# The y of the second mixture's second group, and the first block of the tail, moved in among the expert items

## The chip, the cores and the metric

The kernel runs on one core of a Trainium2 chip. The metric is the device time of one execution in microseconds (us). Engines are named as in the profile: PE is TensorE, DVE VectorE, ACT ScalarE, POOL GpSimd, SP SyncE; PEld is TensorE's loading of weights. Each engine works through its own queue in order.

## The reference

Three stages follow each other: attention in a sliding window, a mixture of eight experts, and a wide layer with g(h) = h cos h ("second mixture" here). All is float32, and the weights of the last layer come as float64.

```
x = softmax(mask(q k^T / 8 - slope |i - j|)) v        # 4 batches, 8 heads, 576 rows, window 128
x = x as 2304 rows of 512
e = argmax(x w_gate + modality_bias[modality_id])     # 8 experts
out[t] = gate[t] * (relu(x[t] w1[e]) w2[e])           # w1 512 x 1024, w2 1024 x 512
h = out w_in                                          # 512 x 2048
y = (h * cos(h)) w_out                                # 2048 x 512
```

## The kernel before

Every product of two float32 matrices is made of three: each operand is split into a high half, a cast to fp32r, and a low half, the rest; TensorE then does high x high, high x low and low x high. A split is so always a cast on ScalarE and a subtraction on VectorE.

**The expert items.** After attention the 2304 rows are sorted by expert into nine items of up to 256 rows each, and a remainder of blocks of up to 128 rows. The loop over `steps` (line 1087) has 72 steps, (item, f) with f over the eight slices of 128 hidden columns, and two more that only finish. Step n does the up products of slice f (`up`, twelve products of 256 columns, tiles `xT` and `s`) and, LAG = 2 steps behind, the down products (`down`, twelve, tiles `hh` and `s`). Two slices make a piece of weights: `load_w` loads `r1` and `r2` (512 KB each, two buffers of each), `split_w1` and `split_w2` split them into `s1s` (three tiles) and `s2s` (two). After a piece's second up, `hh` gets its high half (relu on ScalarE) and low half (VectorE). At an item's end `store_y` copies its four banks and stores y; the place in DRAM is known only at run time, so a later read of y waits for every earlier store. Among the steps 10 to 56 `convert` also turns the first half of the second mixture's float64 weights into `wi_a` and `wo_a` (`from_f64`, line 101: mag and lf on ScalarE, top on VectorE, lf times mag on GpSimd). From step 12 to 66 (`InOrder`) the instructions of each engine stand as the code has them; later a scheduler places them.

**The first block** (`unit_parts`, line 902) is the remainder's first, 128 rows with the roles turned: x is the stationary operand and products have 512 columns. `load_d(p)` loads one eighth of the expert's weights (p 0 to 3 from w1, 4 to 7 from w2), `split_d(p)` splits it into `sds[p]`, `up_d(p)` does six products; after p = 1 and p = 3 the hidden half is taken out with relu (`hr`), `turn` transposes it on TensorE and splits it into `hh2`, `down_d(p)` does six products of the second layer, `end` transposes and stores. The raw weights go to five tiles `raw` of their own; the splits stand at steps 70 to 73, up_d from step 72 on, the rest behind the loop. Other blocks run in a loop of which the count is read at run time (line 1152); here it is not entered.

**The second mixture.** The rows are in five groups of 512 (the last of 256). For group g `fetch_y` (line 861) loads a 128-row tile of y and its gates (`yg`, `gb`), `load_y` (line 868) multiplies them on GpSimd and splits the product into `yT`. In segments of a group and half the weights, `up2` does twelve products of 512 columns (`yT`, `wi_a` or `wi_b`) and the chain of h cos h: ki on ScalarE, two steps of r on VectorE, abs and sin on ScalarE, a product on VectorE, then `gg`, high half on ScalarE and low half on VectorE. `down2` does twelve products two steps behind (`wo_a`, `gg`). The second half of the weights, `wi_b` and `wo_b`, is converted during the first three segments. Before the change group 0 is fetched in steps 66 to 69 of the items, group 1 in the second mixture's own first steps.

## Time and profile before

| what | us |
|---|---|
| runs of the kernel | 871.32, 872.38, 876.11 (median 872.38) |
| the profiled execution | 872.53 |
| its span, first to last instruction | 870.8 |
| TensorE busy in it | 823.5 (95%) |
| VectorE busy | 631.9 (73%) |
| ScalarE busy | 529.2 (61%) |
| GpSimd busy | 223.4 (26%) |
| mean granted TensorE clock | 0.987 |

Times in the rows are us from the span's start. The items run from about 200 to 437 us, the first block ends at 454, the second mixture fills the rest. A start in an order of time is where an instruction began; "x12" are twelve that were merged, and what is in brackets is the time that the engine stood idle before it and what ended that.

### The profile page before, as it was taken

The numbers are of one execution on the slowest core, as the hardware profiler recorded it, in microseconds if no ns is written. First come the engines' busy times: TensorE is split into PE (matmuls) and PEld (weight loads), VectorE is DVE, ScalarE is ACT, GpSimd is POOL, SyncE is SP. The second block draws the span as 40 slices with busy tenths as digits, with TensorE's granted clock in tenths as the row PEclk, the third lists the DMA queues.
The fourth block names the chain that finished last, engine by engine and source line by source line (L and its number), as shares of the span: only waits on it lengthen the run. The fifth ranks groups of instructions, "written<-read, shape, count | busy, mean of one in ns | idle before, by whom it ended". The sixth has DMA issues, their size and how long they took to land. (4 is left out here: it accounts for less than half of the span.)

```text
span 870.8 us, 14990 instructions
## 1 busy us (share of the span) xinstructions
PE 823.5 (95%) x5269; PEld 728.1 (84%) x5269; DVE 631.9 (73%) x1492; ACT 529.2 (61%) x980; POOL 223.4 (26%) x283
## 2 busy tenths in 40 slices
PE   6899999987989999999987999999999999999996
PEld 6789988976889999999966888887788888888895
DVE  4877778767879999897646999998665565545562
ACT  6988788844556666664535776664544555445562
POOL 6665565320112223221113211111313001200000
PEclk9999999997999999999998999999999999999999
DMA  7354442018578877856824131410402000100000
GB/s 159 95 139 110 117 109 75 32 42 261 182 254 263 299 269 266 277 197 208 293 85 140 51 132 60 153 65 25 133 19 91 1 1 21 53 1 0 25 26 24
DMA packets 125137, 103.43 MB, mean 119 GB/s; under 512 B 61725, under 2 KB 105027, under 8 KB 125059
## 3 DMA queue, kind: packets, MB, share of 16 engines
q1 hardware_dynamic: 122099, 92.74, 34.6%
q0 software_dynamic: 2960, 9.70, 3.2%
q8 instruction: 42, 0.69, 0.3%
q14 instruction: 36, 0.29, 0.1%
HBM read 85.90 MB, written 16.52 MB: 118 GB/s over the span
## 5 line engine op out<-in xcount | busy, mean ns | idle before, releaser
L973 PE MATMUL bk<-hh,s 128*128 128x256 f32 x864 | 121.8, 287 | 7.9 <-DVE hh L973 7.1
L973 PEld LDWEIGHTS bk<-hh,s 128*128 128x128 f32 x864 | 109.7, 191 | 12.0 <-DVE hh L973 10.3
L973 PE MATMUL bk<-xT,s 128*128 128x256 f32 x864 | 117.2, 285 | 1.4 <-ACT s L973 0.9
L973 PE MATMUL bk<-wo_a,gg 128*128 128x512 f32 x432 | 110.0, 402 | 4.4 <-ACT gg L973 3.8
L973 PEld LDWEIGHTS bk<-xT,s 128*128 128x128 f32 x864 | 109.9, 193 | 1.9 <-ACT s L973 1.0
L973 PE MATMUL bk<-yT,wi_b 128*128 128x512 f32 (+1 forms) x480 | 107.3, 372 | 0.0
L973 PE MATMUL bk<-yT,wi_a 128*128 128x512 f32 (+1 forms) x480 | 106.3, 372 | 0.5 <-PEq L1152 0.5
L973 DVE TENSOR_TENSOR s<-r,s 128x1024 fp32r<-128x1024 f32 x72 | 93.6, 1303 | 17.8 <-ACT s L973 17.4
L973 PE MATMUL bk<-wo_b,gg 128*128 128x512 f32 x432 | 104.9, 392 | 0.5 <-ACT gg L973 0.3
L973 ACT ACTIVATE r<-r 128x512 f32<-128x512 f32 (+1 forms) x80 | 47.1, 589 | 94.8 <-DVE r L973 94.4
L973 POOL TENSOR_TENSOR lf<-lf,mag 128x512 f32<-128x512 f32 x32 | 46.3, 1446 | 218.8 <-DVE mag L973 194.1
L973 PEld LDWEIGHTS bk<-wo_a,gg 128*128 128x128 f32 x432 | 81.9, 192 | 24.0 <-ACT gg L973 4.7
L973 ACT CAST s<-r 128x1024 fp32r<-128x1024 f32 x72 | 75.3, 1052 | 42.4 <-DMA r<-in_moe_w_dram 33.8
L973 PEld LDWEIGHTS bk<-yT,wi_a 128*128 128x128 f32 x480 | 85.0, 190 | 17.5 <-ACTq L1152 0.7
L973 PEld LDWEIGHTS bk<-yT,wi_b 128*128 128x128 f32 x480 | 84.8, 188 | 17.6
L973 PEld LDWEIGHTS bk<-wo_b,gg 128*128 128x128 f32 x432 | 80.5, 188 | 19.2 <-ACT gg L973 0.8
L973 DVE TENSOR_TENSOR r<-bk,r 128x512 f32<-128x512 f32 (+1 forms) x80 | 51.0, 637 | 60.2 <-ACT r L973 59.8
L973 DVE TENSOR_TENSOR gg<-r,gg 128x512 fp32r<-128x512 f32 (+1 forms) x80 | 55.9, 699 | 36.8 <-ACT gg L973 36.5
L973 ACT CAST gg<-r 128x512 fp32r<-128x512 f32 (+1 forms) x80 | 46.1, 577 | 46.6 <-DVE r L973 45.4
L712 PE MATMUL bk<-vt,pT 128*128 128x65 f32 x544 | 71.8, 275 | 1.9 <-POOL pT L686 0.8
L712 PEld LDWEIGHTS bk<-vt,pT 128*128 128x128 f32 x544 | 67.8, 195 | 3.2 <-issue 1.5
L973 DVE SCALAR_TENSOR_TENSOR r<-ki,bk 128x512 f32<-128x512 int32 (+1 forms) x80 | 50.5, 631 | 23.6 <-ACT ki L973 23.3
(279 smaller groups left out, 1380.0 us busy)
## 6 DMA issues: line engine op xcount, KB each, us to landing
r<-in_moe_w_dram SPq DMA_DIRECT2D x72, 512.0 KB
f64w<-in_moe_w_in_dram SPq DMA_DIRECT2D x14, 512.0 KB
f64w<-in_moe_w_out_dram SPq DMA_DIRECT2D x13, 512.0 KB
y_dram<-y SPq DMA_DIRECT2D x19, 256.0 KB
yg<-y_dram SPq DMA_DIRECT2D x18, 256.0 KB
rqk<-in_q_dram SPq DMA_DIRECT2D x32, 128.0 KB
rqk<-in_k_dram SPq DMA_DIRECT2D x32, 128.0 KB
vt<-in_v_dram SPq DMA_DIRECT2D x32, 128.0 KB
```

The costliest lines, as they stand in the source:

```text
L712: nc.tensor.matmul(ot[:, h, 0:65], pT[b], vt_of(bp, t0 + b, hg)[:, 65 * h:65 * h + 65], start=b == 0, stop=b == nv - 1)
L973: r = op(*args, **kwargs)
```

## The change

Five things are moved.

1. `load_y` of group 0 goes from steps 68 to 71 to steps 46 to 49, and group 1's from the second mixture to steps 66 to 69. The fetches stand two steps ahead of each (44 and 64). The tile `yT1` takes the memory that `raw` had.
2. The block's raw weights use the items' own buffers `r1` and `r2`: four buffers for eight loads, `load_d` at steps 66, 67, 68 and 70, the other four as a split frees a buffer.
3. `split_d` of p = 0 and 1 stand at steps 68 and 70, `up_d` of p = 0 and 1 at steps 70 and 71, the next two and `turn(0)` among steps 72 and 73. `hr` is kept in the tiles `xgs`, which held gathered x.
4. The second mixture opens with four up products; then two down products, and from there it is two steps behind as it was. The banks for h are four in turn instead of three. The first two float64 conversions there wait two steps longer after their load.
5. The copies of partial sums that go to DRAM are all on ScalarE; half were on VectorE.

```diff
-        nc.sync.dma_start(raws[p % len(raws)], src.rearrange("o (j p) d -> p (o j) d", p=128))
+        r = RAW["d", p] = rp_.tile([128, 2, DM], F32, name="rd", tag="r%d" % (1 + p // 2 % 2), bufs=2)
+        nc.sync.dma_start(r, src.rearrange("o (j p) d -> p (o j) d", p=128))
...
+    sds = sds[:4] + sds[:3] + sds[4:]
...
-        w, r = sds[p % len(sds)], raws[p % len(raws)]
+        w, r = sds[p], RAW.pop(("d", p))
...
-        if p + len(raws) < 8:
-            load_d(p + len(raws))
+        if p < 4:
+            load_d(p + 4)
...
-                hr[h] = gp.tile([128, DM], F32, name="hr", tag="y")
+                hr[h] = xgs[1 - h]
...
-        return [part((up_d, 0)), part((up_d, 1)), part((split_d, 4), (up_d, 2), (split_d, 5), (turn, 0)),
-                part((up_d, 3), (split_d, 6)), part((down_d, 4), (split_d, 7), (turn, 1)), part((down_d, 5)),
-                part((down_d, 6)), part((down_d, 7)), part((end,))]
+        return {"begin": [part((up_d, 0)), part((up_d, 1))],
+                "among": [(part((split_d, 2), (split_d, 3), (turn, 0)), part((up_d, 2), (split_d, 4))),
+                          (part(), part((up_d, 3), (split_d, 5)))],
+                "end": [part((down_d, 4), (turn, 1), (split_d, 6), (split_d, 7)), part((down_d, 5)), part((down_d, 6)),
+                        part((down_d, 7)), part((end,))]}
...
-        N0, N1 = len(steps) - 5, len(steps) - 10
+
+        N0, N1, N2 = 44, len(steps) - 10, len(steps) - 8
...
-        SPLIT_AT = [-2, -1, 0, 1]
         first = unit_parts()
+        LOAD_AT, SPLIT_AT, BEGIN_AT = {66: 0, 67: 1, 68: 2, 70: 3}, {68: 0, 70: 1}, (70, 71)
...
-            if 0 <= n - N0 + 1 < groups[0][1]:
-                fetch_y(0, n - N0 + 1, gp)
-            if 0 <= n - N0 - 1 < groups[0][1]:
-                load_y(0, n - N0 - 1, ytiles[0])
+            for g, n0 in enumerate((N0, N2)):
+                if 0 <= n - n0 < groups[g][1]:
+                    fetch_y(g, n - n0, gp)
+                if 0 <= n - n0 - 2 < groups[g][1]:
+                    load_y(g, n - n0 - 2, ytiles[g])
...
-            if n >= len(steps):
-
-                first.pop(0)()
+
+            if n in SPLIT_AT:
+                split_d(SPLIT_AT[n])
+            if n in BEGIN_AT:
+                first["begin"].pop(0)()
+            among = first["among"].pop(0) if n >= len(steps) else (lambda: None,) * 2
+            among[0]()
             if n >= LAG:
                 down(*steps[n - LAG])
+            among[1]()
+            if n in LOAD_AT:
+                load_d(LOAD_AT[n])
...
-        conv = Steps([lambda f=f, fn=fn, w=w: fn(NA + f, w[1][:, 0, f], w[1][:, 1, f], cv, f64w, 0)
-                      for f, fn, w in turns if 0 <= f < NA])
+        conv = Steps([lambda n=n, f=f, fn=fn, w=w: fn(NA + f, w[1][:, 0, f], w[1][:, 1, f], cv, f64w, 2 if n < 2 else 0)
+                      for n, (f, fn, w) in enumerate(t for t in turns if 0 <= t[0] < NA)])
...
-            ph = bank("SST"[i % 3], [128, 512])[:, :w]
+            ph = bank("SSTT"[i % 4], [128, 512])[:, :w]
...
-                        (nc.scalar.copy if j % 2 else nc.vector.tensor_copy)(o, ACC[s][j])
+                        (nc.scalar.copy if j % 2 or f1 < NF2 else nc.vector.tensor_copy)(o, ACC[s][j])
...
-            if i >= LAG and (s < NS - 1 or f < LAG or f >= TAIL):
+
+            if i > LAG and (s < NS - 1 or f < LAG or f >= TAIL):
+                if i == LAG + 1:
+                    down2(*downs.pop(0))
                 ins = down2(*downs.pop(0))
```

What this does to the order on the engines is shown at three places. The first is VectorE in steps 46 to 49 (s1 and s2 are halves of the items' weights, hh the hidden tile that TensorE waits for, mag, top and wo_a belong to a float64 conversion). Before:

```order
L973 TENSOR_SCALAR mag_5711<-top_5752 128x512
L973 TENSOR_TENSOR s1_1_3776<-r1_5745,s1_1_3776 128x1024
L973 TENSOR_TENSOR top_5752<-top_5752,wo_a_3767 128x512
L132 TENSOR_TENSOR wo_a_3767<-top_5752,lf_5753 128x512
L973 SCALAR_TENSOR_TENSOR hh_5844<-bk_5797,hh_5844 128x512
L973 TENSOR_TENSOR s2_0_3778<-r2_5674,s2_0_3778 128x1024
L973 TENSOR_SCALAR mag_5830<-mag_5830 128x512
L973 TENSOR_SCALAR top_5862<-mag_5830 128x512
L973 SCALAR_TENSOR_TENSOR top_5862<-f64w0_3789,top_5862 128x512
L973 TENSOR_TENSOR s1_2_3777<-r1_5822,s1_2_3777 128x1024
L973 TENSOR_SCALAR mag_5830<-top_5862 128x512
L973 SCALAR_TENSOR_TENSOR hh_5914<-bk_5869,hh_5914 128x512
```

and after:

```order
L974 TENSOR_SCALAR mag_5711<-top_5756 128x512
L974 TENSOR_TENSOR yT0_3771<-yg_5733,yT0_3771 128x4x128
L974 TENSOR_TENSOR s1_1_3776<-r1_5749,s1_1_3776 128x1024
L974 TENSOR_TENSOR top_5756<-top_5756,wo_a_3767 128x512
L974 SCALAR_TENSOR_TENSOR hh_5859<-bk_5805,hh_5859 128x512
L974 TENSOR_TENSOR yT0_3771<-yg_5785,yT0_3771 128x4x128
L132 TENSOR_TENSOR wo_a_3767<-top_5756,lf_5757 128x512
L974 TENSOR_TENSOR s2_0_3778<-r2_5674,s2_0_3778 128x1024
L974 TENSOR_SCALAR mag_5845<-mag_5845 128x512
L974 TENSOR_SCALAR top_5884<-mag_5845 128x512
L974 SCALAR_TENSOR_TENSOR top_5884<-f64w0_3789,top_5884 128x512
L974 TENSOR_TENSOR yT0_3771<-yg_5818,yT0_3771 128x4x128
```

Three of four splits of y (yT0) stand in these rows, the fourth right behind the next hh; each waits for a product on GpSimd. The end of the float64 weight (wo_a) now stands behind the hh that it was ahead of.

The second is TensorE from step 70 to the branch (xT_94 and hh with 256 columns are the last item, s with xT_95 and 512 columns is up_d, s with hh and a number is down_d, ident are the transposes of turn and end). Before:

```order
L973 MATMUL bk<-xT_94,s_2_3777 128x256 x12
L973 MATMUL bk<-hh,s_0_3778 128x256 x12
L973 MATMUL bk<-s_0_3775,xT_95 128x512 x6
L973 MATMUL bk<-hh,s_1_3779 128x256 x12
L973 MATMUL bk<-s_1_3776,xT_95 128x512 x6
L973 MATMUL bk<-hh,s_1_3779 128x256 x12
L973 MATMUL bk<-s_2_3777,xT_95 128x512 x6
L973 MATMUL bk<-ident,hr 128x128 x4
L973 MATMUL bk<-s_0_3778,xT_95 128x512 x6
L973 MATMUL bk<-s_1_3779,hh_6872 128x512 x6
L973 MATMUL bk<-ident,hr 128x128 x4
L973 MATMUL bk<-s_0_3775,hh_6872 128x512 x6
```

and after:

```order
L974 MATMUL bk<-xT_94,s_2_3777 128x256 x12
L974 MATMUL bk<-s_0_3775,xT_95 128x512 x6
L974 MATMUL bk<-hh,s_0_3778 128x256 x12
L974 MATMUL bk<-xT_94,s_2_3777 128x256 x12
L974 MATMUL bk<-s_1_3776,xT_95 128x512 x6
L974 MATMUL bk<-hh,s_0_3778 128x256 x12
L974 MATMUL bk<-ident,xg_97 128x128 x4
L974 MATMUL bk<-hh,s_1_3779 128x256 x12
L974 MATMUL bk<-s_2_3777,xT_95 128x512 x6
L974 MATMUL bk<-hh,s_1_3779 128x256 x12
L974 MATMUL bk<-s_0_3778,xT_95 128x512 x6
L974 MATMUL bk<-s_0_3775,hh_6851 128x512 x6
```

The two first sets of up_d stand between the last item's own products, and no set of transposes is followed at once by the products that need it.

The third is ScalarE after the branch, at the opening of the second mixture (ki, r and gg are the chain of h cos h; mag and lf belong to the float64 weights). Before:

```order
L973 ACTIVATE ki<-bk 128x512
L973 ACTIVATE r<-r 128x512
L973 ACTIVATE r<-r,hpi 128x512
L973 ACTIVATE ki<-bk 128x512
L973 ACTIVATE mag<-f64w 128x512
L973 CAST gg<-r 128x512
L973 ACTIVATE mag<-f64w 128x512
L973 ACTIVATE ki<-bk 128x512
L973 ACTIVATE r<-r 128x512
```

and after:

```order
L974 ACTIVATE ki<-bk 128x512
L974 ACTIVATE lf<-f64w 128x512
L974 ACTIVATE r<-r 128x512
L974 ACTIVATE r<-r,hpi 128x512
L974 ACTIVATE ki<-bk 128x512
L974 CAST gg<-r 128x512
L974 ACTIVATE ki<-bk 128x512
L974 ACTIVATE r<-r 128x512
L974 ACTIVATE r<-r,hpi 128x512
```

The two mag are gone from these rows, and one lf stands right behind the first ki.

## Rows read from the trace of the kernel before

**Rows 1.** Stretches: us of it; busy us (instructions) of five engines; granted clock; DMA.

```profile
346.00:368.00 22.00, 21.52 (x180) 21.11 (x179) 21.09 (x30) 15.13 (x22) 6.95 (x5) 1.00 0.82 275
...
427.00:455.00 28.00, 23.12 (x136) 18.76 (x135) 16.66 (x19) 13.01 (x20) 5.85 (x4) 1.00 0.38 120
455.00:482.00 27.00, 22.56 (x84) 17.42 (x83) 17.45 (x28) 14.00 (x24) 7.14 (x5) 0.87 0.40 123
```

**Rows 2.** TensorE's waits from 425 to 480: us in total, times, longest.

```profile
PE bk L973 <- ACT gg L973: 3.8, 2, 3.1
PE bk L973 <- ACT hr L973: 1.8, 2, 1.1
```

**Rows 3.** Order of time on TensorE, step 70 to the branch: start, us, operation.

```profile
427.03 1.58 PE L973 MATMUL bk<-xT,s 128*128 128x256 f32 x12
...
438.42 1.59 PE L973 MATMUL bk<-hh,s 128*128 128x256 f32 x12
439.85 1.55 PE L973 MATMUL bk<-s,xT 128*128 128x512 f32 x6
...
448.09 0.60 PE L973 MATMUL bk<-ident,hr 128*128 128x128 f32 x4
448.44 4.38 PE L973 MATMUL bk<-s,hh 128*128 128x512 f32 x18
...
454.65 8.41 PE L973 MATMUL bk<-yT,wi_a 128*128 128x512 f32 x36 [0.46 <-PEq L1152]
```

**Rows 4.** Order of time on SyncE around the branch.

```profile
454.95 0.37 SPq L946 DMA_DIRECT2D y_dram<-y  x1
458.69 0.39 SPq L144 DMA_DIRECT2D f64w<-in_moe_w_in_dram  x1
```

**Rows 5.** Order of time on ScalarE, opening of the second mixture.

```profile
459.79 0.63 ACT L973 ACTIVATE r<-r 128x512 f32<-128x512 f32 x1 [1.48 <-DVE r L973]
...
462.52 0.67 ACT L973 ACTIVATE mag<-f64w 128x512 f32<-128x512 f32 x1 [0.86 <-DMA f64w<-in_moe_w_in_dram]
463.10 0.60 ACT L973 CAST gg<-r 128x512 fp32r<-128x512 f32 x1
467.38 0.66 ACT L973 ACTIVATE mag<-f64w 128x512 f32<-128x512 f32 x1 [3.67 <-DMA f64w<-in_moe_w_in_dram]
```

**Rows 6.** Order of time on TensorE, opening of the second mixture.

```profile
472.69 0.73 PE L973 MATMUL bk<-wo_a,gg 128*128 128x512 f32 x2 [3.12 <-ACT gg L973]
...
478.48 3.71 PE L973 MATMUL bk<-yT,wi_a 128*128 128x512 f32 x12
482.03 2.95 PE L973 MATMUL bk<-wo_a,gg 128*128 128x512 f32 x12
484.81 2.89 PE L973 MATMUL bk<-yT,wi_a 128*128 128x512 f32 x12
```

**Rows 7.** The stretch right behind the longest gap, columns as in rows 1.

```profile
474.00:476.00 2.00, 1.95 (x5) 1.58 (x6) 1.97 (x4) 1.31 (x3) 0.20 (x1) 0.50 0.07 21
```

**Rows 8.** The tile yg: duration in ns (least, median, longest), first and last start.

```profile
L973 POOL TENSOR_TENSOR yg<-yg,gb x18: 1283/1292/2052, 429.7 to 745.2; 128x512 f32<-128x512 f32 x18
...
L973 DVE TENSOR_TENSOR yT<-yg,yT x18: 678/684/1121, 431.6 to 790.4; 128x512 fp32r<-128x512 f32 x18
```

**Rows 9.** Groups of instructions, 340 to 400 us: busy us, mean ns, idle before.

```profile
L973 DVE TENSOR_TENSOR s<-r,s 128x1024 fp32r<-128x1024 f32 x19 | 25.9, 1363 | 3.3 <-ACT s L973 3.2
...
L973 DVE TENSOR_TENSOR top<-top,wo_a 128x512 f32<-128x512 f32 x7 | 5.9, 837 | 0.0
```

**Rows 10.** Order of time on VectorE, steps 46 to 52.

```profile
357.85 1.78 DVE L973 TENSOR_TENSOR top<-top,wo_a 128x512 f32<-128x512 f32 x1
359.74 0.69 DVE L132 TENSOR_TENSOR wo_a<-top,lf 128x512 fp32r<-128x512 f32 x1
...
370.25 1.23 DVE L973 TENSOR_TENSOR s<-r,s 128x1024 fp32r<-128x1024 f32 x1 [1.86 <-ACT s L973]
```

**Rows 11.** Order of time on ScalarE, step 51.

```profile
369.17 1.05 ACT L973 CAST s<-r 128x1024 fp32r<-128x1024 f32 x1 [2.06 <-DMA r<-in_moe_w_dram]
```

More of the change, by code (lines that the diff above doesn't have):

```diff
@@ L874, in load_y @@
         nc.vector.tensor_tensor(yT[:, 1, :, cs], yg, yT[:, 0, :, cs].bitcast(F32), op=ALU.subtract)
-    ctx_d = ctx.enter_context(ExitStack())
-    raws = []
     def load_d(p):
@@ L938, in end @@
             r = nc.sync.value_load(regs[0:1, NL + MIN_ITEMS:NL + MIN_ITEMS + 1], min_val=0, max_val=NT)
-            yr = gp.tile([128, DM], F32, name="hr", tag="y")
+            yr = xgs[1]
             nc.scalar.copy(yr, acc[0])
@@ L984 @@
     nc = Engines
+    rps = hc.enter_context(ExitStack())
+    rp_ = pool(rps, "rp", 2, "right")
     with ExitStack() as c:
-        rps = c.enter_context(ExitStack())
-        rp_ = pool(rps, "rp", 2, "right")
         cvs = c.enter_context(ExitStack())
@@ L1120 @@
                 cvs.close()
-                dp = pool(ctx_d, "dp", 1)
-                raws += [dp.tile([128, 2, DM], F32, name=f"raw{j}") for j in range(5)]
-            if N1 < n <= N1 + len(raws):
-                load_d(n - N1 - 1)
+                yt1 = pool(ctx, "yt1", 1)
+                ytiles.append(yt1.tile([128, 2, KD * 512], F32R, name="yT1"))
             if n == len(steps) - 1:
                 splits(len(pieces), len(pieces))
-            if n - len(steps) in SPLIT_AT:
-                split_d(SPLIT_AT.index(n - len(steps)))
-            if n >= len(steps):
-                first.pop(0)()
+            if n in SPLIT_AT:
[4 more added lines that the diff above has]
+            among[0]()
             if n >= LAG:
                 down(*steps[n - LAG])
+            among[1]()
+            if n in LOAD_AT:
+                load_d(LOAD_AT[n])
             with ExitStack() as later:
@@ L1141 @@
                     convert(n)
-        for part in first:
+        for part in first["end"]:
             part()
         InOrder.on = False
-        rps.close()
     n_units = nc.values_load(regs[0:1, 2 * NL:2 * NL + 1], min_val=0, max_val=UNITS,
@@ L1160 @@
             gather(MIN_ITEMS, 0)
-            for p in range(len(raws)):
+            for p in range(4):
                 load_d(p)
             to_xT(MIN_ITEMS, 0)
-            for p in range(4):
+            parts = unit_parts()
+            for p in range(2):
                 split_d(p)
-            for part in unit_parts():
+            for part in parts["begin"] + [p for two in parts["among"] for p in two] + parts["end"]:
                 part()
@@ L1170 @@
     rc.close()
-    ctx_d.close()
-    yt1 = pool(ctx, "yt1", 1)
-    ytiles.append(yt1.tile([128, 2, KD * 512], F32R, name="yT1"))
     with ExitStack() as c:
@@ L1270 @@
             for j in range(groups[g][1]):
-                if s and (s == 1 or f0 == 0):
-                    at = 0 if s == 1 else i0 - 8
-                    fetches.setdefault(at + j, []).append((g, j))
-                    loads.setdefault(at + 2 + j, []).append((g, j))
+                if g > 1:
+                    fetches.setdefault(i0 - 8 + j, []).append((g, j))
+                    loads.setdefault(i0 - 6 + j, []).append((g, j))
                 if f0:
```

## The prediction

> **What bounds the kernel now.** I read the busy times by stretch first, then TensorE's waits, then the order of time on TensorE, ScalarE, VectorE and SyncE around them. TensorE is the bound nearly everywhere, so a change pays only where TensorE stands idle or runs at a lower clock, and costs wherever it makes TensorE wait anew. The stretches [rows 1] tell two stories. From 346 to 368 us (steps 44 to 50 of the items) TensorE is busy 21.52 of 22 us and VectorE 21.09: two engines full at once. From 427 to 455 us (end of the items and the first block) TensorE is idle 4.9 us, and from 455 to 482 us (opening of the second mixture) 4.4 us, with the granted clock at 0.87 on average. The longest waits there [rows 2] are 3.8 us for the high half of gg and 1.8 for the block's hidden values (hr). The change is aimed at these stretches.
>
> **The block, steps 70 on.** TensorE starts step 70 at 427.03 and the mixture at 454.65 [rows 3]: 27.6 us. Twelve 256-column products take 1.43 us at full pace (438.42 to 439.85 [rows 3]), six 512-column ones 1.39 (half of twelve, 482.03 to 484.81 [rows 6]), four transposes 0.35 (448.09 to 448.44 [rows 3]). The stretch holds six of the first (8.6), eight of the second (11.1) and three of the third (1.1): 20.8. So 6.8 us are lost: the gaps, and the drain of the pipeline at each. After the change two up products stand between the items' own, and turn(0) and turn(1) have other products around them, so relu, cast and split hide beside 1.4 us or more of products. What stays is the end (the shorter of the two waits for hr, 0.7 [rows 2], and 0.46 at the branch [rows 3], with drain some 1.7). What is new: the first split needs a load that leaves only at step 66, behind item 7's stores and a fetch of y that needs them landed. Step 65 ends near 415.2 (four steps of 2.86 and one transposition before 427.03). The second copy of y now stands on ScalarE behind a split that waits for its own load, so I put the second store at 418.5, an estimate. SyncE passes on 3.7 us after a store (454.95 to 458.69 [rows 4]), so 422.2, and the load leaves at about 422.8. A load of 512 KB takes 3.8 us (458.69 until ScalarE has it at 462.52 [rows 4, 5]): 426.6, up to 427.5 with others in flight. A cast of 1.05 [rows 11] and a split of 1.23 [rows 10] give the low half at 428.9 to 429.8, where TensorE wants it at 428.9: 0 to 0.9, I take 0.8. The eighth load waits until the fourth split has freed its buffer, and the last split then makes the second hidden tile late by some 1.4 us. With 0.2 at the first turn the new loss is 1.7 + 0.8 + 1.4 + 0.2 = 4.1 us. **Gain 6.8 - 4.1 = 2.7 us.** Bounds: 5.1 (only the end stays) and 0.3 (the loads 2.4 us later, two thirds of a load's length).
>
> **The opening.** From 454.65 [rows 3] to the fourth set of down products at 482.03 [rows 6] TensorE does seven sets of twelve, 84 products of 512 columns. At 2.78 us a set that is 19.5 us; it takes 27.4. Of the lost 7.9, 4.4 are gaps, one of them 3.12 long [rows 6], and after it the granted clock stands at 0.50, the lower of the two levels [rows 7]: a set of up products takes 3.55 us there (478.48 to 482.03), and some 6 us at half pace lose 3.1. The gaps come from ScalarE: its abs for the second float64 weight (mag) waits for a load until 467.38 [rows 5] and holds everything of the second and third gg behind it. Now the fetches of y that were in that load's way have moved, the two abs stand later, and four sets of up products cover 11.1 us. One wait is new: ScalarE has the low words of the first float64 weight (lf) right behind the first ki, before the first r. SyncE sends that load only at 458.69, 4.0 us after the branch, and it is there at 462.52, 7.9 after. Without the wait r starts at 459.79, 5.1 after the branch; with a lf like the mag of 0.67 it starts 8.5 after. From r's start to the end of the first gg it took 3.9 us, of which mag waited 0.86 and stood 0.58 in the way [rows 5]; so 2.5 to 3.1, and gg's high half comes 11.0 to 11.6 after the branch, where TensorE wants it at 11.1. The second gg follows along the same chain some 4.4 us later, at 15.6, an estimate; TensorE is done with the first down set at 14.2. So the waits are 0.3 and 1.4, with drains and a late low half 2.4 in all. **Gain 7.9 - 2.4 = 5.5 us**, if the clock stays up: the block's gaps of up to 1.1 us left it at 1.00 [rows 1, 2], the one of 3.12 did not. Bounds: 7.2 (load early) and 2.4 (clock falls: 3.1 less).
>
> **The items.** Eight load_y now lie among the items: the first four in steps 46 to 49, the second four in 66 to 69, where VectorE has room. In the first place it has none, idle 0.9 us of 22 [rows 1]. Each load_y adds 1.29 us on GpSimd and 0.68 on VectorE [rows 8], 0.60 from start to start. And GpSimd's products hold VectorE up where both inputs lie in SBUF: the top at 357.85 takes 1.78 us instead of 0.69 [rows 10], and over 340 to 400 us the 19 splits take 1363 ns instead of 1220, the seven such tops 837 instead of 690 [rows 9], in sum 3.7 us for six products of GpSimd, 0.6 each. So VectorE gets 4 x 0.60 + 4 x 0.6 = 4.8 us more before the hh of steps 46 to 50. It can give back the 1.86 us of idle time at 370.25 [rows 10], which ended with a cast that had waited 2.06 us for weights [rows 11], and TensorE's slack at one hh, an estimated 0.5: TensorE ends 2.4 us later. This is not won back, TensorE being the bound after it. The fetches (1 MB), whose second pair waits on SyncE for the first pair's split, delay weights by a microsecond or two within this. At step 61 one cast of y stands ahead of an hh on ScalarE: 0.4 more. **Loss 2.8 us.** Bounds: 0.8 (idle time takes most of it) and 6.5 (nothing given back, and a load late by 1.3).
>
> By the Trainium skill (SBUF — State Buffer, Who interferes with whom) the pair of ports that the two engines share is locked for a whole instruction, so the later one blocks fully. The rows agree with it in kind. Taken at its worst, each of GpSimd's products would block VectorE its whole length, and the forecast would come out 2.8 us higher.
>
> The rest is at nothing: copies of partial sums moved to ScalarE, which is busy 14.0 of 27 us from 455 to 482 [rows 1] while TensorE has products to do; a fourth bank in the later segments, which moves products on TensorE but adds none; hidden tiles in the xgs buffers, which are read out by then.
>
> **Sum**, against the profiled execution's own 872.53 us (span 870.8; the median of the runs is 872.38, 0.15 lower): 872.53 - 2.7 - 5.5 + 2.8 = 867.1 us, 0.6% below the median. About 0.5%, 4.4 us, is what a measurement here can tell from no change: faster is under 868.0, slower over 876.7.
>
> **Rivals.**
> (1) The items hide the load of y: loss 0.8, and block gain 3.5. Then 872.53 - 3.5 - 5.5 + 0.8 = 864.3. For it: VectorE's splits run up to two pieces ahead. Against: TensorE waits for hh right there, and VectorE has 0.9 us free. Chance 0.25.
> (2) The wait for lf takes the place of the one for mag: the first gg comes later than four sets cover, TensorE stands long enough that the clock falls again, opening gain 2.4: 870.2. For it: the load cannot leave before 458.69. Against: 11.1 us of cover. Chance 0.17.
> (3) The change does not do what it says, the block begins no sooner in effect: its loads queue behind stores and fetches, each up product waits, block gain 0.3: 869.5. For it: eight loads now pass through four buffers, two of a kind. Chance 0.13.
> (4) Slower: GpSimd's products and the fetches on SyncE's queue starve the items. Each product blocks VectorE for all its 1.29 us, 4 x 1.29 + 2.4 = 7.6, nothing is given back, and a load of weights that stands behind a fetch adds its 3.8: the items lose 11.4. It decides as soon as the items lose more than the 8.2 us gained; then 872.53 - 8.2 + 11.4 = 875.7. For it: VectorE is full. Against: 0.6, not 1.29, is what a product costs now. Chance 0.08.
> The forecast itself has 0.37, spread 865 to 870.
>
> **How the numbers follow.** Likeliest 867.1. The low end takes rival 1 with more of the block and opening: 872.53 - 4.2 - 6.6 + 0.8 = 862.5. The high end, 874.0, lies past rivals 2 and 3 together (872.6) and short of rival 4; about one in ten is left out at either end. Faster by over 0.5%: rival 1 (0.25), and four fifths of the forecast's 0.37 (0.30): 0.55. Slower by over 0.5%: the upper part of rival 4, 0.05. The rest, 0.40, is no change.
>
> **What would show it.** Right: TensorE's gaps from step 70 to the branch add up to 2 to 4 us, and the branch comes 2 to 3 us sooner after step 70; the opening has its first gap of note at the second down set, under 2 us, with the clock at 1.00; ScalarE's lf waits there for a float64 load about 4 us; TensorE waits for hh in steps 46 to 52 some 2.5 us more in sum. Wrong: a granted clock of 0.50 after the branch, an up product of the block that waits over 2 us for a load, or items that lose under 1 or over 6 us.

## The result, and the profile of the changed kernel

The changed kernel takes 876.68 us (median of 20 runs) beside 871.93 for the kernel before on the same chips: the ratio is 1.0052 with the 95% interval 1.0036 to 1.0068, half a per cent slower. The prediction was 867.1 us, faster. The profiled execution took 875.33 us (span 873.6), 2.8 more than the 872.53 of before.

By the prediction's own split the 2.8 us are these. From the start of step 44 to that of step 70 the items lost 9.0 us less 0.2 gained ahead of them; the block, from step 70 to the branch, gained 0.3; the opening and what follows gained 5.7: 9.0 - 0.2 - 0.3 - 5.7 = 2.8. The opening came out as forecast (5.5), the block at its lower bound, and the items at three times their term (2.8).

To find the place, I mark time by ScalarE's high half of hh, one every two steps. Four stretches are used in all tables from here on: the **first place** (hh of step 41 to hh of step 55, where the first group's load_y now stands), the **second place** (55 to 69), the **block** (69 to the branch) and the **rest** (branch to the end of the span). This block begins at ScalarE's hh and not at TensorE's step 70. In the changed kernel that hh comes 0.7 us later against step 70 than before, so 0.7 passes from the one to the other here: the two places lose 9.8 where the items lose 9.0, and the block gains 1.0 where it gains 0.3 from step 70.

| kernel | first | second | block | rest |
|---|---|---|---|---|
| before | 44.9 | 42.6 | 28.0 | 416.1 |
| changed | 51.8 | 45.5 | 27.0 | 410.4 |

The first place alone lost 6.9 us. The busy times of the two kernels there, PE, PEld, DVE, ACT, POOL with their counts, then the granted clock, the share of the DMA engines and GB/s; first before, then after, and of after also the stretches 366 to 370 and 370 to 380:

```profile
339.09:384.02 44.93, 43.34 (x359) 42.49 (x358) 41.74 (x59) 29.58 (x43) 11.03 (x8) 1.00 0.74 247
```

```profile
338.92:390.74 51.82, 45.89 (x355) 44.55 (x354) 49.16 (x63) 31.86 (x47) 17.42 (x12) 0.93 0.73 241
366.00:370.00 4.00, 2.73 (x24) 2.53 (x22) 3.93 (x6) 2.22 (x5) 2.64 (x2) 1.00 0.81 239
370.00:380.00 10.00, 7.78 (x40) 7.28 (x41) 9.14 (x14) 4.36 (x7) 1.27 (x1) 0.66 0.81 283
```

VectorE had 41.7 busy of 44.9 us and has 49.2 of 51.8: its work grew by 7.4 us and the stretch by 6.9. TensorE is busy 2.55 us more with the same products, since its clock fell (0.66 on average from 370 to 380); the other 4.3 us it stood. Where it stood, in the order of time on TensorE of after:

```profile
362.81 1.58 PE L974 MATMUL bk<-hh,s 128*128 128x256 f32 x11 [1.24 <-DVE hh L974]
...
369.93 0.39 PE L974 MATMUL bk<-hh,s 128*128 128x256 f32 x1 [1.27 <-ACT y L974]
371.54 0.70 PE L974 MATMUL bk<-hh,s 128*128 128x256 f32 x2 [1.23 <-DVE hh L974]
373.24 2.29 PE L974 MATMUL bk<-hh,s 128*128 128x256 f32 x9 [1.00 <-DVE y L974]
375.33 2.76 PE L974 MATMUL bk<-xT,s 128*128 128x256 f32 x12
```

Three gaps of 1.0 to 1.3 us lie within five microseconds here, and one of 1.24 ends six before them. Behind them a set of twelve takes 2.76 us in place of 1.58: the granted clock is 1.00 up to 370, 0.92 from 370 to 372 and 0.50, the lower of its two levels, from 372 to 378. So it fell behind the gaps of 1.27 and 1.23 us, before the last one had ended. Two of the gaps wait for `y`, the copies that free item 5's banks for item 6. ScalarE's order of time shows one of these copies waiting for the split of a tile yg: `store_y` and `fetch_y` take their tiles from the same two buffers of the pool gp, both named "y".

```profile
369.51 0.37 ACT L974 COPY y<-bk 128x256 f32<-128x256 f32 x1
372.93 0.37 ACT L974 COPY y<-bk 128x256 f32<-128x256 f32 x1 [3.05 <-DVE yT L974]
```

The same sharing stands behind the block. Item 7's second store needs the buffer of the first one's, and SyncE's queue has the block's loads behind it:

```profile
423.55 4.31 SPq L853 DMA_DIRECT2D y_dram<-y  x2
429.49 0.40 SPq L1001 DMA_DIRECT2D r<-in_moe_w_dram  x1
430.00 0.40 SPq L865 DMA_DIRECT2D yg<-y_dram  x1
430.59 0.38 SPq L886 DMA_DIRECT2D rd<-in_moe_w_dram  x1
```

The first load leaves 7.6 us after the start of step 66 (422.99), as the prediction had it; TensorE then waits 0.31 and 1.47 us for the first split where 0.8 was reckoned, and the clock falls once more (0.94 over the block):

```profile
435.91:463.19 27.28, 23.66 (x134) 19.78 (x133) 16.67 (x18) 14.29 (x20) 1.28 (x1) 0.94 0.46 160
463.19:490.00 26.81, 25.47 (x107) 19.77 (x108) 16.03 (x28) 14.80 (x25) 1.30 (x1) 1.00 0.24 75
```

The second line is the opening: clock 1.00, TensorE idle 1.3 us. Its one gap is 1.25 us at the second down set, after lf had waited 4.01 us for its load, both as named beforehand.

### The profile page after: what moved, and what is told of

Its sections match the earlier page's. It is cut to its first block, busy times and chain, and to the rows that moved or that the text cites. A ratio compares the mean times of both kernels' runs of the same rounds, so it can differ in the third digit from the quotient of the medians.

```text
span 873.6 us, 14987 instructions
## 1 busy us (share of the span) xinstructions
PE 824.4 (94%) x5269; PEld 728.4 (83%) x5269; DVE 633.3 (72%) x1488; ACT 530.9 (61%) x984; POOL 222.4 (25%) x283
## 5 line engine op out<-in xcount | busy, mean ns | idle before, releaser
L974 PE MATMUL bk<-hh,s 128*128 128x256 f32 x864 | 124.1, 291 | 13.1 <-DVE hh L974 8.5
L974 PEld LDWEIGHTS bk<-hh,s 128*128 128x128 f32 x864 | 112.1, 194 | 17.4 <-DVE hh L974 11.0
L974 POOL TENSOR_TENSOR lf<-lf,mag 128x512 f32<-128x512 f32 x32 | 45.2, 1414 | 255.8 <-DVE mag L974 243.2
L974 PE MATMUL bk<-wo_a,gg 128*128 128x512 f32 x432 | 107.9, 396 | 1.3 <-ACT gg L974 1.3
L974 DVE TENSOR_TENSOR s<-r,s 128x1024 fp32r<-128x1024 f32 x72 | 95.5, 1330 | 16.7 <-ACT s L974 15.1
L974 ACT ACTIVATE r<-r 128x512 f32<-128x512 f32 (+1 forms) x80 | 47.1, 589 | 89.6 <-DVE r L974 89.6
```

What stands on the lines that cost most here:

```text
L974: r = op(*args, **kwargs)
```

## What the experiments asked

Two theories stood against each other. **A**: the y tiles come too late or hold buffers that the stores need, so it is a matter of buffers and order. **B**: VectorE, full already, is blocked by GpSimd's products and given more to do, whatever the buffers. **C**, a third: the fetches on SyncE's queue make the weights late. All runs in one table; a ratio is to the kernel before on the same chip, the stretches are from each kernel's profile (us), and DVE is VectorE's busy time in the first place. Each stretch is from one execution only. The five kernels named late have the same code up to the hh of step 55, and their first place takes 43.8 to 45.3 us, so a difference of up to 1.5 us in a stretch can be chance. The kernels own, own_nogate, own_b_nogate and fetch_only leave something out or read wrong data, and serve only to measure.

| kernel | median | ratio (95%) | first | DVE | second | block | rest |
|---|---|---|---|---|---|---|---|
| before | 871.9 | 1 | 44.9 | 41.7 | 42.6 | 28.0 | 416.1 |
| changed | 876.7 | 1.0052 (1.0036 to 1.0068) | 51.8 | 49.2 | 45.5 | 27.0 | 410.4 |
| own | 874.5 | 1.0006 (0.9982 to 1.0029) | 53.6 | 47.1 | 47.0 | 25.5 | 411.4 |
| n0_42 | 875.6 | 1.0024 (1.0006 to 1.0042) | 51.6 | 45.9 | 45.4 | 26.0 | 411.4 |
| n2_59 | 873.3 | 1.0000 (0.9990 to 1.0010) | 52.3 | 49.0 | 43.9 | 23.6 | 410.2 |
| own_nogate | 870.7 | 0.9964 (0.9943 to 0.9985) | 48.4 | 44.4 | 45.2 | 23.2 | 411.3 |
| own_b | 873.5 | 0.9999 (0.9977 to 1.0021) | 50.7 | 48.6 | 45.8 | 25.1 | 410.4 |
| own_b_nogate | 868.2 | 0.9935 (0.9902 to 0.9968) | 47.8 | 44.5 | 44.7 | 23.5 | 411.5 |
| own_b_n2 | 868.7 | 0.9949 (0.9926 to 0.9972) | 51.2 | 49.1 | 42.8 | 23.6 | 410.9 |
| no_open | 875.4 | 1.0035 (1.0014 to 1.0056) | 52.5 | 48.9 | 44.9 | 26.1 | 409.7 |
| fetch_only | 865.2 | 0.9922 (0.9900 to 0.9943) | 47.0 | 40.0 | 43.0 | 23.9 | 410.8 |
| own_b_n2_dve | 871.6 | 0.9985 (0.9972 to 0.9998) | 52.2 | 46.7 | 43.7 | 24.7 | 411.7 |
| late | 870.6 | 0.9978 (0.9960 to 0.9995) | 45.1 | 41.0 | 51.3 | 23.7 | 410.8 |
| late_noopen | 868.1 | 0.9950 (0.9930 to 0.9970) | 43.8 | 41.4 | 51.1 | 23.7 | 409.7 |
| late_gb4 | 868.8 | 0.9950 (0.9927 to 0.9973) | 45.3 | 41.1 | 49.2 | 23.6 | 410.6 |
| own_b_n2_gb4 | 870.6 | 0.9946 (0.9926 to 0.9967) | 51.5 | 49.0 | 43.0 | 23.6 | 411.6 |
| own_b_n2_noopen | 869.5 | 0.9946 (0.9927 to 0.9966) | 52.0 | 49.1 | 42.6 | 23.6 | 409.7 |
| late_gb4_noopen | 868.8 | 0.9949 (0.9930 to 0.9968) | 44.2 | 40.5 | 49.4 | 23.6 | 410.9 |
| late_gb8 | 868.1 | 0.9944 (0.9924 to 0.9964) | 43.8 | 40.4 | 47.6 | 23.6 | 410.8 |

## Experiments on the buffers

**own** gave the fetched tiles two buffers of their own, in memory that had been the third buffer of the float64 weights.

```diff
-        yg = YG[g, j] = yp.tile([128, KD, 128], F32, name="yg", tag="y")
+        yg = YG[g, j] = ygs[j % 2] if yp is gp else yp.tile([128, KD, 128], F32, name="yg", tag="y")
```

> The changed kernel, but the gated tiles yg that are fetched among the items have two buffers of their own (memory taken from the third float64 buffer); in the changed kernel they share the two buffers y of the items' stores. Theory A (shared buffers: item 5's copies at step 49 and item 7's at step 65 wait until load_y gives a buffer back): steps 50 to 52 lose the 3.5 us of standing and the some 2 us of low clock, the first block's loads leave about 2 us sooner, 875.3 - 5.5 - 2 = 868 (866 to 870). Theory B (VectorE and GpSimd block each other, and VectorE has more to do, whatever the buffers): the lost 9 us stay, 874 to 876. Theory C (the fetches on SyncE's queue and the DMA traffic make the weights late): the same as B, 874 to 876.

Measured: 874.5 us, the first place 53.6. The edit was a poor one: the fetch of tile j + 2 stands ahead of load_y of tile j, so in two fixed buffers it overwrote two of the four tiles in each of the first two groups, and their load_y waited for a fetch two tiles on. So it doesn't tell the theories apart, though the time lies in the range of B and C.

**n0_42** moved the first group two steps sooner (`N0 = 42`), clear of item 5's store.

> The changed kernel with the first group's fetches and load_y two steps sooner (fetch 42 to 45, load_y 44 to 47): the last yg is split before item 5's copies at step 49, the buffers stay shared. Theory A: the standing at steps 50 to 52 and the low clock behind it go, 5.5 of the 9 us; the second place (step 65) stays: 870 (868.5 to 871.5). Theories B and C: the same work on VectorE, GpSimd and SyncE in an equally full stretch, only sooner: 874 to 876.

Measured: the first place still loses 6.6 us, though no copy waits for a split any more. ScalarE, n0_42:

```profile
354.20 0.62 ACT L974 CAST yT<-yg 128x512 fp32r<-128x512 f32 x1 [5.04 <-POOL yg L974]
...
356.25 0.58 ACT L974 ACTIVATE hh<-bk 128x512 fp32r<-128x512 f32 x1
```

The two fetches now wait for item 4's stores to land, leave at 347.06, and the cast of y, which stands in order ahead of hh, waits 5.0 us for GpSimd's product of what they bring. So the sharing of buffers was one way to the loss, and taking it away opened another; A as stated (870 us) missed by 5. The time lies in the range of B and C (874 to 876), but not by B's way alone: VectorE is busy only 45.9 of 51.6 us there, and stands 3.6 us until a cast of y is done.

**n2_59** moved the second group five steps sooner (fetch 59 to 62, load_y 61 to 64), ahead of item 7's store.

> The changed kernel with the second group's fetches and load_y five steps sooner (fetch 59 to 62, load_y 61 to 64), so that item 7's copies at step 65 find no yg in their buffers; the first group stays. Theory A: what the late stores cost behind step 65 comes back, 1.1 us at steps 66 to 68 and 2 us of the first block, 872.3 (871 to 873.5); steps 50 to 52 lose as before. Theory B: the work of VectorE is the same, 874.5 to 876.

Measured: 0.5% below the changed kernel, the second place 43.9 and the block 23.6. Theory A's range holds the time, and the gain by the trace is more than it said: 1.6 us in the second place, 3.4 in the block. The earlier steps do two things at once, though. They clear the buffers for the store, and they take the casts of y away from ahead of step 69's hh and the fetches from ahead of the block's loads, so the run doesn't price the sharing by itself.

**own_b** kept the steps and gave two of each group's four tiles memory of their own (`... if yp is gp and j // 2 != g else ...`), **own_b_n2** moved the second group as well.

> The changed kernel with its steps as they are, but of each group two of the four fetched tiles yg lie in memory of their own (taken from the third float64 buffer), so that no fetch waits for a split and the last yg of the first group isn't in the way of item 5's store. Theory A (y comes too late for its place: ScalarE's cast and VectorE's split of y stand in order ahead of hh and wait for it, and the stores wait for the buffer): the standing at steps 50 and 51 and the low clock behind it go, some 5.5 of the 9 us lost: 870 (868 to 872). Theory B (VectorE has too much to do, and GpSimd's products block it): the work is the same, 874.5 to 877.

> As own_b, and the second group five steps sooner (fetch 59 to 62, load_y 61 to 64), clear of item 7's store at step 65. Theory A: both places are mended; n2_59 alone brought the branch 4 us sooner than in the changed kernel by the trace (459.15 against 463.19), so this comes out 2 to 4 us below own_b, 867 (865 to 869). Theory B: the same work, 873 to 877.

Measured: in the first place own_b wins 1.1 us of 6.9 and own_b_n2 0.6, VectorE being about as busy as in the changed kernel (48.6 and 49.1 us). Theory A falls for the first place: no copy waits for a split there, and 5.8 and 6.3 us are lost all the same. Instead a cast of wo_a, ahead of hh on ScalarE, waits 3.53 and 3.16 us for VectorE's top (1.63 in the changed kernel). The time of own_b lies between the two ranges; own_b_n2 comes out in A's (865 to 869), by the second place and the block alone, where it has n2_59's gain: 42.8 and 23.6. In own_b, with the second group at its late steps, the second place doesn't gain (45.8) and the block 1.9 us; a cast of y on ScalarE ahead of step 69's hh waits 3.44 us there. The block of own_b_n2, with the loads leaving from 424.0 on, before step 70 begins at 432.76:

```profile
432.76:456.22 23.46, 21.84 (x134) 18.66 (x133) 13.10 (x15) 11.22 (x16) 0.00 (x0) 1.00 0.45 152
```

23.5 us from step 70 to the branch instead of 27.6: a gain of 4.2, near the prediction's upper bound of 5.1.

## Experiments on the products

**own_nogate** and **own_b_nogate** left GpSimd's eight products out.

```diff
-        nc.gpsimd.tensor_tensor(yg, yg, GB.pop((g, j)).to_broadcast([128, KD, 128]), op=ALU.mult)
+        gb = GB.pop((g, j))
+        if g > 1:
+            nc.gpsimd.tensor_tensor(yg, yg, gb.to_broadcast([128, KD, 128]), op=ALU.mult)
```

> As own, but GpSimd's eight products of y with the gates among the items are left out (y of the first two groups stays without its gate); the fetches, casts and splits stay. This measures what GpSimd's products cost the items once the buffers are apart. Theory A: VectorE's time blocked by them (0.6 us each, 4 of them where VectorE is full) is part of what is left, 1 to 2.5 us below own. Theory B: they are the main cost, each holding VectorE 1.29 us and more: 5 us or more below own. If TensorE's slack hides them: within 0.7 us of own.

> As own_b, but GpSimd's eight products of y with the gates among the items are left out (y of the first two groups stays without its gate); fetches, casts and splits stay. It shows what the products cost. Theory A: the casts no longer wait the 1.3 us for the product, and VectorE is blocked 0.6 us less four times: 1 to 2.5 us below own_b. Theory B: the products are the main cost, 5 us or more below own_b. If TensorE's slack hides them: within 1 us of own_b.

Measured: own_nogate, which keeps own's fault in the fetches, comes 3.8 us below own; own_b_nogate comes 5.3 below own_b, in the first place 2.9. VectorE's groups there, line, shape and count, busy time and mean ns of one, idle time before them; before, then after (GpSimd's products in a fence of their own), then own_b_nogate, and last the busy times of the first place in own_b_n2 and in own_b_nogate:

```profile
L973 DVE TENSOR_TENSOR s<-r,s 128x1024 fp32r<-128x1024 f32 x15 | 20.5, 1368 | 2.9 <-ACT s L973 2.8
```

```profile
L974 DVE TENSOR_TENSOR s<-r,s 128x1024 fp32r<-128x1024 f32 x15 | 22.7, 1512 | 2.4 <-ACT s L974 2.4
...
L974 DVE TENSOR_TENSOR yT<-yg,yT 128x512 fp32r<-128x512 f32 x4 | 4.6, 1146 | 0.0
L132 DVE TENSOR_TENSOR wo_a<-top,lf 128x512 fp32r<-128x512 f32 x5 | 4.5, 902 | 0.1
```

```profile
L974 POOL TENSOR_TENSOR yg<-yg,gb 128x512 f32<-128x512 f32 x4 | 6.8, 1702 | 4.2 <-DMA yg<-y_dram 3.0 <-DVE hh L974 1.2
```

```profile
L976 DVE TENSOR_TENSOR s<-r,s 128x1024 fp32r<-128x1024 f32 x15 | 21.4, 1425 | 3.1 <-ACT s L976 3.0
```

```profile
338.57:389.78 51.21, 45.81 (x356) 44.38 (x355) 49.10 (x63) 31.56 (x47) 17.41 (x12) 0.93 0.78 254
```

```profile
339.54:387.33 47.79, 44.79 (x355) 43.59 (x354) 44.49 (x63) 31.54 (x47) 11.52 (x8) 0.96 0.82 267
```

Without the products VectorE's work is 44.5 - 41.7 = 2.75 us more than before, four bare splits of 0.69. With them it is 4.1 to 4.7 more again (own_b 48.6 with one split fewer in the window, own_b_n2 49.1, changed 49.2): each product takes 1.0 to 1.2 us of VectorE's time where the prediction had 0.6. This is so where VectorE hardly ever stands; in own against own_nogate, where it stands 6.5 us of 53.6, the four products take 2.7 us, 0.7 each. A split of y takes 1146 ns on average in the changed kernel, where the median before was 684 [rows 8], the last sums of wo_a 902 where they took 688 before, a split of weights 1512 and 1425 without the products; the products themselves grow from 1292 [rows 8] to 1702 ns. Not all of it is the moved products: without them one split of y still takes 1.45 us, beside GpSimd's product for a float64 weight. The times fit theory B for own_b_nogate (5 us or more) and lie between the two ranges for own_nogate.

**own_b_n2_dve** let VectorE multiply.

```diff
-        nc.gpsimd.tensor_tensor(yg, yg, GB.pop((g, j)).to_broadcast([128, KD, 128]), op=ALU.mult)
+        (nc.gpsimd if g > 1 else nc.vector).tensor_tensor(yg, yg, GB.pop((g, j)).to_broadcast([128, KD, 128]), op=ALU.mult)
```

> As own_b_n2, but the eight products of y with the gates among the items are made by VectorE, 0.6 us each from start to start, and not by GpSimd. With the eight products left out altogether own_b_nogate stood 5.3 us below own_b. Theory B1 (the price is that GpSimd and VectorE block each other): most of it comes back although VectorE has more to do, 868.7 - 3 = 865.5 (864.5 to 867). Theory B2 (the price is VectorE's fullness, whoever multiplies): no gain or a loss, 868 to 870.

Measured: 3 us above own_b_n2, the way of theory B2 and past its range (868 to 870). VectorE's busy time falls (46.7), so the blocking is less, but the stretch doesn't: the cast on ScalarE now waits for VectorE's queue, 10.1 us in sum from 350 to 385.

```profile
ACT yT L974 <- DVE ob L974: 5.4, 2, 2.8
ACT yT L974 <- DVE yg L974: 4.7, 2, 2.6
```

**fetch_only** left of the first group only the transfers, doubled: y goes straight into both halves of yT, with no product, cast or split.

```diff
+        if g == 0:
...
+            for a in range(2):
+                nc.sync.dma_start(v[:, a, :, cs].bitcast(F32), y_dram[:, :, cs])
+            return
```

> As own_b_n2, but of the first group only the transfers stand among the items: each tile of y goes straight into both halves of yT by two DMAs at steps 46 to 49, with no product, cast or split (group 0 stays without its gate and unsplit; the transfers are doubled). The first place (hh of step 41 to hh of step 55) took 44.9 us before and 51.2 in own_b_n2. Theory B (the instructions of load_y on GpSimd, ScalarE and VectorE are the price): 45 to 46 us there, 868.7 - 5.5 = 863. Theory C (fetches on SyncE's queue and DMA traffic): it stays over 49 us, 867 to 869.

Measured: 865.2 us; the first place 47.0, 2.1 us above before and so one above theory B's 45 to 46. So of own_b_n2's 6.3 us lost there, some 4.2 are load_y's instructions; by own_b_nogate 3 or so are the products. The transfers have a part in the rest, some 2.1 at double their number, two steps later and without the rows of gates. Theory C is so a small share here. Both kernels have two float64 buffers in place of three, but late, with two as well, has 45.1 in the first place, so that isn't the price.

## Experiments on the opening

**no_open** took the opening's own edits back (two sets of up products ahead, three banks, no delay of the first float64 weights); the same on other kernels: **late_noopen**, **own_b_n2_noopen**, **late_gb4_noopen**.

```diff
-            if i > LAG and (s < NS - 1 or f < LAG or f >= TAIL):
-                if i == LAG + 1:
-                    down2(*downs.pop(0))
+            if i >= LAG and (s < NS - 1 or f < LAG or f >= TAIL):
```

> The changed kernel with the opening of the second mixture as it was before (two up products ahead, three banks in turn, the first two float64 weights not delayed); the moved y and the moved block stay. The trace of the changed kernel gives its opening 5.7 us over the kernel before. If the gain comes from the opening's own edits: 876.7 + 5 = 881.5 (880 to 883). If it comes from the fetches of y that left the opening: within 1.5 us of the changed kernel, 876 to 878.

> As late, with the opening of the second mixture as it was before (two up products ahead, three banks, first float64 weights not delayed). no_open against the changed kernel gave no loss, so the gain of the opening should come from the fetches of y that left it: within 1.5 us of late. If the opening's own edits hide something once the kernel is faster: 2 us or more above late.

> As own_b_n2, with the opening of the second mixture as it was before the change. By the traces, the time from the branch to the end was 410.4 us in the changed kernel against 409.7 in no_open, and 410.8 in late against 409.7 in late_noopen: the opening's own edits cost 0.7 to 1 us, and so this comes out at 867.7 (866.7 to 868.5). If the edits are worth what the prediction gave them: 871 or more.

> As late_gb4, with the opening as it was before the change: 0.7 to 2.4 us below late_gb4, 865.5 (863.5 to 867), the fastest of all if the gates' buffers are worth 4 us.

Measured: from the branch to the end 409.7, 409.7, 409.7 and 410.9 us without the edits, 410.2 to 411.7 in the kernels with them. They are worth nothing that can be told apart from a loss of up to one us; as ratios the pairs differ by 0.28% (late), 0.17% (changed) and 0.03% or less (the two others). The forecasts of the single times mostly missed: late_noopen came 2.5 us below late where 1.5 was the bound, own_b_n2_noopen 1.0 and late_gb4_noopen 1.8 us above their ranges; only the reading that the edits bring nothing held in all four. Item 5 of the change, the copies moved to ScalarE, was not taken back in any run. TensorE in no_open, in order of time from the branch:

```profile
463.74 8.41 PE L974 MATMUL bk<-yT,wi_a 128*128 128x512 f32 x36 [0.46 <-PEq L1156]
472.81 3.06 PE L974 MATMUL bk<-wo_a,gg 128*128 128x512 f32 x12 [0.66 <-ACT gg L974]
475.70 2.93 PE L974 MATMUL bk<-yT,wi_a 128*128 128x512 f32 x12
478.47 2.96 PE L974 MATMUL bk<-wo_a,gg 128*128 128x512 f32 x12
```

The gap of 3.12 us [rows 6] is gone with the old order too. By the trace, what took it away is that both float64 loads leave together, no fetch of y between them, and the second mag waits 0.26 us where it waited for a load until 467.38 before [rows 5]:

```profile
467.54 0.96 SPq L144 DMA_DIRECT2D f64w<-in_moe_w_in_dram  x2
```

```profile
473.01 0.68 ACT L974 ACTIVATE mag<-f64w 128x512 f32<-128x512 f32 x1 [0.26 <-DMA f64w<-in_moe_w_in_dram]
```

## Experiments on the place

**late** moved the first group's load_y to steps 58 to 61, where VectorE had 11 us free, and the second group's to 62 to 65 (`N0, N1, N2 = 56, len(steps) - 10, 60`, own memory for the first two tiles of each group).

> As own_b_n2, but the first group's load_y not in steps 46 to 49, where VectorE is full, but in 58 to 61, where the float64 conversions thin out, and the second group's in 62 to 65. Theory B (work put where VectorE has no room): the first place costs as before the change, 6.3 us less than in own_b_n2, the later steps 1 to 2.5 us more: 868.7 - 6.3 + 1.8 = 864.2 (862.5 to 866). If the same work costs the same anywhere among the items (A, the in-order chain alone): 868 to 869.5.

Measured: 870.6, above both ranges. The first place is as before (45.1), but the second loses 8.7 us: the loss moved with load_y. VectorE isn't full there (38.3 of 51.3 us busy). SyncE stood at a fetch of gates for a product on GpSimd, and ScalarE waited for the weights behind it (sum, times, longest; from 386 to 434):

```profile
SPq L866 <- POOL ob L974: 10.3, 3, 8.6
```

```profile
ACT s L974 <- DMA r<-in_moe_w_dram: 6.2, 3, 4.2
```

The gates' rows have two buffers for four tiles. **late_gb4** gave them four, **late_gb8** a place for each of the eight rows, in tiles of the routing; **own_b_n2_gb4** tried four in the first place. The edit of late_gb8:

```diff
-        gb = GB[g, j] = yp.tile([128, 1, 128], F32, name="gb", bufs=2)
+        gb = GB[g, j] = gbs(4 * g + j) if yp is gp and 4 * g + j > 1 else yp.tile([128, 1, 128], F32, name="gb", bufs=2)
```

> As late, with four buffers for the rows of gates (gb) among the items in place of two, so that no fetch of gates waits on SyncE's queue for a product on GpSimd, with the weights behind it. If that wait is what made late lose 8.7 us from the hh of step 55 to that of step 69: the 4.2 us for which ScalarE waited for weights go, 870.6 - 4 = 866.6 (865 to 868). If it is the in-order chain of product, cast and split itself: 869.5 to 871.5.

> As own_b_n2, with four buffers for the rows of gates. In the first place VectorE is busy 49.1 of 51.2 us, so, if VectorE is the bound there, a shorter queue on SyncE changes nothing: 868.7, within 1 us. If the queue on SyncE (4.2 us at gates in this stretch) had a part in it: 1.5 to 3 us less.

> As late, with a place of its own for each of the eight rows of gates, so that SyncE's queue never stands at gates until a product on GpSimd is done. Late lost 8.7 us from the hh of step 55 to that of step 69, late_gb4 6.6. If the weights queued behind that hold are the cause: ScalarE's waits for weights there (8.6 us in late_gb4) fall under 5, the stretch loses 2 to 4 us, 868.8 - 3.5 = 865.3 (864 to 867). If the products, casts and splits in their order are the cause: 868 to 870, as late_gb4.

Measured: late_gb4 won 2.0 us in the second place, but SyncE still stood 8.7 us at a gate row, now one of the second group that had been issued early. late_gb8 has no such wait any more, ScalarE waits less for weights (4.6 us from 384 to 434, late 6.2, late_gb4 8.6), and the second place comes to 47.6: 3.7 us of late's 8.7 were the hold on SyncE's queue. The total, 868.1, still lies in the range of the other reading (868 to 870, the products, casts and splits in their order), so this hold is less than half of the loss.

```profile
ACT s L974 <- DMA r<-in_moe_w_dram: 4.6, 4, 2.5
```

The first place doesn't care (own_b_n2_gb4 51.5 against 51.2; its median, 870.6, is 0.9 us above the range). Of late_gb8's second place VectorE is busy 41.6 of 47.6 us; how the 5.0 us that remain divide stays open. late_gb8 is the fastest kernel that computes all, 0.56% under the kernel before and 1.07% under the changed one; own_b_n2 and its relatives follow at 0.5%, too near to be told from it.

## Why the prediction was wrong, step by step

**The items** are the step that failed: 2.8 us forecast, 9.0 measured, beyond the upper bound of 6.5 and past the sign of being wrong that was named, a loss of over 6. In the first place two terms were mis-sized and one was missing.

- GpSimd's products were priced at 0.6 us of VectorE each, from a mean over 60 us of before [rows 9] in which six products met whatever VectorE happened to do. In a stretch where VectorE stands only 2.1 to 2.7 of 51 us, it is 1.0 to 1.2.
- The 1.86 us of VectorE's idle time and 0.5 of slack were to be given back. They were not: VectorE's idle time in the first place went from 3.2 to 2.7 us. The 1.86 did go, but other idle time came, 0.76 us behind the copy of y that had waited 3.05 and 0.78 behind a cast that waited for TensorE's product. With the measured price and only these 0.5 given back, the sum reads 2.75 + 4.7 - 0.5 = 6.9, what the first place lost. This is VectorE's busy and idle time added up, and so proves nothing by itself; that the products cause the larger part is what own_b_nogate and fetch_only show. Nor is VectorE's work the whole story: n0_42 and own_b_n2_dve lose 6.6 and 7.3 us with VectorE 4.2 and 5.0 busier, where casts of y, in order ahead of other work on ScalarE, wait 5.04 us and, in sum, 10.1.
- The clock had no place in the term. Here it fell behind gaps that lie close together, and TensorE is busy 2.55 us longer with the same products. How much the slower pace adds to VectorE's lateness isn't shown: in own_b TensorE is only 1.3 us busier than before, and the first place still loses 5.8.

Another 2.9 us by ScalarE's hh (2.2 by TensorE's start of step 70) fell in the second place, where 0.4 was given. The cast at step 61 waited 3.56 us for its product, and hh comes 1.1 us later by step 63. The other 1.8 come behind item 7's store, late by a yg in its buffer: TensorE waits 0.84 us for its copy, and a cast of y ahead of step 69's hh waits 3.28 for its product. That `fetch_y` and `store_y` share the two buffers "y" stands in the code, and the prediction did not see it. n2_59 wins 5.0 us with the block by moving the second group out of the store's way; how much of it is the sharing and how much the order of the casts stays open, own_b having won 1.9 in the block and nothing in the second place.

**The block**: 2.7 us forecast, 0.3 measured, the lower bound and the time of rival 3. The hour of the first load was right to 0.1 us by luck: the second store left 4.5 us after the start of step 66 and not 3.3, late by its buffer, and SyncE passed on sooner than the 3.7 us reckoned. The wait for the split was 1.8 and not 0.8, the wait for the last splits' hidden tile 0.65 and not 1.4, and the clock fell, which the term did not have: the rest of up_d's first set and the down set behind it (440.01 to 443.97 us) take some 1.6 us more than at full pace. In own_b_n2, with the loads in time and the second group's y out of the way, the block gains 4.2 at a clock of 1.00, so the mechanism was right and its time of arrival was not.

**The opening**: 5.5 forecast, 5.7 measured, with its one gap and the 4 us wait of lf in their places. But of the three causes named (fetches gone, abs later, four sets ahead) the two later ones bring nothing by no_open, and the first is what the trace leaves.

**The rivals**: 1 fell, 2 did not happen (clock 1.00). 3 (chance 0.13) came true in the block by its number; of the up products only the first waited. 4 (0.08) came true in the items in its first half, GpSimd's product blocking VectorE for most of its length with next to nothing given back, and gave 875.7 us; the profiled execution took 875.33. That the times agree so well is luck: the items lost 9.0 and not 11.4, and the block gained 0.3 and not 2.7. Its second half, weights behind a fetch, was not what the first place lost (ScalarE waits 3.5 us for weights there, 6.1 before), though late showed that it can. Its condition, items losing more than 8.2, was met by 9.0. The chance of 0.05 for slower was too small for a stretch in which two engines are full.

The prediction weighed a rule of the Trainium skill (SBUF — State Buffer, Who interferes with whom): the pair of ports is locked for a whole instruction, and the later one blocks fully. Taken at its worst it put the forecast 2.8 us higher. Where VectorE hardly stands the runs come near that end: four products of 1.29 us would be 5.2 us of VectorE, and 4.1 to 4.7 were measured (2.7 in own, where it stands more). Even so the forecast would have stayed below what was measured, with 5.6 us for the items against 9.0.

## What to carry to other kernels

Where a stretch has an engine full, price what is added there by what that engine's instructions take beside the new neighbour, not by a mean over a calmer stretch, and take no idle time back unless you know what ends it. Before moving a load, list every buffer and every queue that it shares with its new neighbours: here a tile's shared name held a copy for 3.05 us, two rows of gates were 3.7 us of late's loss, and fetches behind a store's landing held a cast for 5.04. A gain that a change ascribes to three edits may belong to one: undo the others before keeping them. A forecast that comes near by time alone may be two errors that cancel: compare it stretch by stretch.

## What was not expected of the hardware

A short VectorE instruction with one input can be held up too: a masking of 128x512 words takes 0.43 us, and 2.07 where GpSimd's product of y begins before its end (own_b, VectorE; own and own_b_n2 show the same 2.07). In the changed kernel, where it lay beside GpSimd's descriptors for a gather alone (at 366.56, the product from 367.37 on), it took 0.43:

```profile
354.80 0.43 DVE L974 TENSOR_SCALAR top<-mag 128x512 int32<-128x512 int32 x1
...
366.94 2.07 DVE L974 TENSOR_SCALAR top<-mag 128x512 int32<-128x512 int32 x1
```

And the granted clock fell in the changed kernel after gaps of which none was longer than 1.27 us, two of them within three microseconds (0.66 on average from 370 to 380 us, 1.00 from 366 to 370). In late a gap of 1.66 us left the pace alone (eleven products in 1.67 us), and behind one of 1.58 us eight microseconds later they took 2.26; what sets the two apart no run here shows:

```profile
392.66 1.67 PE L974 MATMUL bk<-hh,s 128*128 128x256 f32 x11 [1.66 <-DVE hh L974]
400.96 2.26 PE L974 MATMUL bk<-hh,s 128*128 128x256 f32 x11 [1.58 <-DVE hh L974]
```
